# A retention layer in 64-token chunks with a carried state, interleaved with the two layers behind it

## The chip, the cores and the metric

The kernel runs on one core of a Trainium2 chip. The metric is the device time of one execution in microseconds (us), less is better. A core has TensorE (PE), VectorE (DVE), ScalarE (ACT), GpSimd (POOL) and SyncE (SP), each with its own instruction queue that is worked through in order; SP, ACT and POOL also issue DMAs. PEld in the profile is TensorE's loading of weights. SBUF is the on-chip memory, PSUM the memory that matmuls write.

## What is computed

A retention layer (attention without softmax, with a decay per head and a causal mask), then two linear layers with a leaky relu between them. 8 batches, 8 heads, 576 tokens, 64 elements per head, so 4608 tokens of width 512; the hidden width is 2048. Inputs and output are float32, and matmuls run in float16.

```python
scores = scale * np.matmul(q, k.transpose(0, 1, 3, 2))
gamma = 1.0 - 2.0 ** (-5.0 - np.arange(H, dtype=np.float32))
rel = pos[:, None] - pos[None, :]
Dmat = np.where(rel >= 0, gamma[:, None, None] ** rel[None, :, :], 0.0)
x = np.matmul(scores * Dmat[None], v)   # then heads side by side: (4608, 512)
h = x @ w_in                            # (4608, 2048)
g = np.maximum(0.01 * h, h)
out = g @ w_out                         # (4608, 512)
```

## The kernel before

It has two phases, one after the other, and a scheduler sets the order within each engine.

*Before the phases* it loads both weight matrices in float32 over SP's queue (lines 70 and 75) and casts them to float16 on DVE and ACT (71, 77, 79).

*Phase A* (lines 89 to 220) is the retention. It walks over 8 batches x 4 pairs of heads, 32 steps. Two heads share the 128 partitions: `kdiag` and `vdiag` hold the two heads' 64x64 blocks on the diagonal, so that one matmul serves both. A step loads q, k and v of a pair (SP and POOL), casts them (ACT line 130, POOL 131 and 135, ACT 136), transposes q and k on PE (141, 142), and copies the transposes out (145, 147, 151). Then it goes over nine blocks i of 64 keys. A matmul gives the scores of block i with all queries from block i on (185, 200), DVE multiplies them with a table of decays that is zero above the diagonal (192, 207), and two matmuls, which trail by two blocks, add the result times v into `oT0` and `oT1` (163, 170). ACT copies these into `xT` (218, 219), the transposed input of the first layer. So every query block meets every earlier key block.

*Phase B* (lines 222 to 280) goes over nine groups of 512 tokens. For each of 16 blocks `fc` of the hidden width four matmuls make `hps` (235). The leaky relu takes two operations: ACT makes 0.99 relu(h) (243), and DVE adds 0.01 h (247). The second layer's four matmuls of block fc - 1 follow (259), into four PSUM tiles; after the last block they are closed (268), ACT evicts them (277), and SP stores them.

Of the kernel before, what the change touches and what calls it, by code (L numbers as in the profile page):

```python
# [10 lines left out]
FP = mybir.dt.float32  # L11
F16 = mybir.dt.float16


@with_exitstack
def kernel(
# [8 lines left out]
):  # L25
    nc = tc.nc
# [4 lines left out]
    scale = 1.0 / np.sqrt(D)  # L31

    NPAIR = H // 2
    NW = (S + P - 1) // P
    NB = S // 64
    NC = DM // P
    NF = DFF // P
    TOK_G = 512
    NGRP = NT // TOK_G
    NTB = TOK_G // P  # L40

    gamma = 1.0 - 2.0 ** (-5.0 - np.arange(H, dtype=np.float64))
    r_idx = np.arange(P)[:, None]
    c_idx = np.arange(S)[None, :]
    ftab = np.zeros((NPAIR, P, S), dtype=np.float32)
    for p in range(NPAIR):
        gh = np.where(r_idx < 64, gamma[2 * p], gamma[2 * p + 1])
        rr = r_idx % 64
        expo = c_idx - rr
        ftab[p] = np.where(expo >= 0, gh ** np.maximum(expo, 0) * scale, 0.0)  # L50
    f_dram = nc.inline_tensor(ftab.astype(np.float16), name="f2_table")

    const_pool = ctx.enter_context(tc.tile_pool(name="const", bufs=1))
    xt_pool = ctx.enter_context(tc.tile_pool(name="xt", bufs=1))
    w_pool = ctx.enter_context(tc.tile_pool(name="w", bufs=1))
    stage_pool = ctx.enter_context(tc.tile_pool(name="stage", bufs=2))
    diag_pool = ctx.enter_context(tc.tile_pool(name="diag", bufs=1))

    ident16 = const_pool.tile([P, P], F16, name="ident16")
    make_identity(nc, ident16)  # L60

    f2_sb = const_pool.tile([P, NPAIR, S], F16, name="f2_sb")
    nc.sync.dma_start(out=f2_sb, in_=f_dram.ap().rearrange("h a t -> a h t"))

    xT = [xt_pool.tile([P, NT], F16, name=f"xT{r}") for r in range(DM // P)]

    w_in16 = [w_pool.tile([P, DFF], F16, name=f"w_in16_{c}") for c in range(NC)]
    for c in range(NC):
        st = stage_pool.tile([P, DFF], FP, name="w_in_stage")
        nc.sync.dma_start(out=st, in_=moe_w_in[c * P : (c + 1) * P, :])  # L70
        nc.vector.tensor_copy(out=w_in16[c], in_=st)
    w_out16 = [w_pool.tile([P, DM], F16, name=f"w_out16_{f}") for f in range(NF)]
    for f in range(NF):
        st = stage_pool.tile([P, DM], FP, name="w_out_stage")
        nc.sync.dma_start(out=st, in_=moe_w_out[f * P : (f + 1) * P, :])
        if f % 2 == 0:
            nc.scalar.copy(out=w_out16[f], in_=st)
        else:
            nc.vector.tensor_copy(out=w_out16[f], in_=st)

    qk16s = [diag_pool.tile([P, 2, NW, P], F16, name=f"qk16_{z}") for z in range(2)]
    kdiags = [diag_pool.tile([P, 2, NW, P], F16, name=f"kdiag{z}") for z in range(2)]
    vdiags = [diag_pool.tile([P, NB, P], F16, name=f"vdiag{z}") for z in range(2)]
    for z in range(2):
        nc.gpsimd.memset(qk16s[z][64:128, :, 4, :], 0.0)
        nc.gpsimd.memset(kdiags[z], 0.0)
        nc.gpsimd.memset(vdiags[z], 0.0)

    with ExitStack() as phA:
        in_pool = phA.enter_context(tc.tile_pool(name="inp", bufs=2))  # L90
        q2_pool = phA.enter_context(tc.tile_pool(name="q2", bufs=2))
        s2_pool = phA.enter_context(tc.tile_pool(name="s2", bufs=4))
        trq_pool = phA.enter_context(tc.tile_pool(name="trq", bufs=1, space=bass.MemoryType.PSUM))
        trk_pool = phA.enter_context(tc.tile_pool(name="trk", bufs=1, space=bass.MemoryType.PSUM))
        sc_pool = phA.enter_context(tc.tile_pool(name="sc", bufs=2, space=bass.MemoryType.PSUM))
        o0_pool = phA.enter_context(tc.tile_pool(name="o0", bufs=2, space=bass.MemoryType.PSUM))
        o1_pool = phA.enter_context(tc.tile_pool(name="o1", bufs=2, space=bass.MemoryType.PSUM))

        ipb = 0
        for b in range(B):  # L100
            for p in range(NPAIR):
                z = ipb % 2
                hA = 2 * p
                qk_sb = in_pool.tile([P, 2, NW, P], FP, name="qk_sb")
                vd32 = in_pool.tile([P, NB, D], FP, name="vd32")
                for ti, t_ap in enumerate((q, k)):
                    for hh in range(2):
                        nc.sync.dma_start(
                            out=qk_sb[:, ti, 0:4, 64 * hh : 64 * hh + 64],
                            in_=t_ap[b, hA + hh, 0:512, :].rearrange(  # L110
                                "(w t) d -> t w d", t=P
                            ),
                        )
                    nc.sync.dma_start(
                        out=qk_sb[0:64, ti, 4, :].rearrange("t (h d) -> t h d", h=2),
                        in_=t_ap[b, hA : hA + 2, 512:S, :].rearrange(
                            "h t d -> t h d"
                        ),
                    )
# [191 lines left out]
```

## Time and profile before

| | us |
|---|---|
| median of 3 runs (490.32 to 491.0) | 490.34 |
| span of the profiled execution | 488.2 |
| PE busy / DVE / ACT / POOL | 399.5 / 255.2 / 226.6 / 87.5 |
| phase A and loads, by the timeline | 0 to about 211 |
| phase B, by the timeline | about 211 to 484 |

The profile is one execution; a span counts from its first to its last instruction. Matmuls are pipelined and their ends modelled, so the distance between starts, not the busy time of one, says what a matmul costs in a row. In a group's row "xN | busy, mean | idle <-releaser", the idle time is what the engine waited just before these instructions, and the releaser is what ended most of it.

### The profile page before, as it was taken

The numbers are of one execution on the slowest core, as the hardware profiler recorded it, in microseconds if no ns is written. First come the engines' busy times: TensorE is split into PE (matmuls) and PEld (weight loads), VectorE is DVE, ScalarE is ACT, GpSimd is POOL, SyncE is SP. The second block draws the span as 40 slices with busy tenths as digits, with TensorE's granted clock in tenths as the row PEclk, the third lists the DMA queues.
The fourth block names the chain that finished last, engine by engine and source line by source line (L and its number), as shares of the span: only waits on it lengthen the run. The fifth ranks groups of instructions, "written<-read, shape, count | busy, mean of one in ns | idle before, by whom it ended". The sixth has DMA issues, their size and how long they took to land.

```text
span 488.2 us, 6567 instructions
## 1 busy us (share of the span) xinstructions
PE 399.5 (82%) x2336; PEld 203.8 (42%) x2336; DVE 255.2 (52%) x508; ACT 226.6 (46%) x381; POOL 87.5 (18%) x140
## 2 busy tenths in 40 slices
PE   0045788888888888889989899898999989899895
PEld 0023454545555555544434344343444434344341
DVE  2245688888887888883333333333333334334342
ACT  1145567666666666533343433434343343433433
POOL 8212344445444454200000000000000000000000
PEclk9998799999999999999999999999999999999999
DMA  8998798976767766100020200202001020200202
GB/s 305 263 241 215 167 190 190 192 162 149 161 165 165 155 160 160 37 0 1 0 86 2 86 1 1 86 1 86 1 23 64 0 87 1 85 2 0 86 1 86
DMA packets 89520, 47.16 MB, mean 97 GB/s; under 512 B 78736, under 2 KB 80272, under 8 KB 88976
## 3 DMA queue, kind: packets, MB, share of 16 engines
q1 hardware_dynamic: 85392, 37.31, 30.4%
q0 software_dynamic: 4096, 9.44, 7.1%
q8 instruction: 18, 0.29, 0.3%
q14 instruction: 14, 0.11, 0.1%
HBM read 37.29 MB, written 9.44 MB: 96 GB/s over the span
## 4 chain that ended last, share of the span: by engine, by line
PE 67%; DVE 13%; ACT 8%; DMA 5%; issue 3%; SPq 2%; ACTq 0%; DVEq 0%
PE opsum L259 24%; PE hps L235 23%; PE sc L200 10%; DVE s L207 6%; PE oT L163 4%; DVE s L192 4%; ACT qT L145 4%; DMA w_out_stage<-in_moe_w_out_dram 3%; ACT osb L277 2%; PE sc L185 2%; PE trQ L141 2%; DMA w_in_stage<-in_moe_w_in_dram 2%; DVE gt L247 1%; ACT rl L243 1%; PE oT L170 1%
## 5 line engine op out<-in xcount | busy, mean ns | idle before, releaser
L247 DVE SCALAR_TENSOR_TENSOR gt<-hps,rl 128x512 f16<-128x512 f32 x144 | 98.9, 691 | 164.5 <-ACT rl L243 164.2
L243 ACT ACTIVATE rl<-hps 128x512 f16<-128x512 f32 x144 | 85.5, 602 | 154.5 <-PE hps L235 154.5
L259 PE MATMUL opsum<-w_out,gt 128*128 128x512 f16 x540 | 138.5, 379 | 13.8 <-DVE gt L247 13.2
L235 PE MATMUL hps<-xT,w_in 128*128 128x512 f16 x576 | 148.6, 379 | 0.8 <-DVE gt L247 0.8
L207 DVE TENSOR_TENSOR s<-sc,f_sb 128x512 f16<-128x512 f32 (+7 forms) x256 | 106.3, 456 | 14.2 <-PE sc L200 13.7
L200 PE MATMUL sc<-qT,kdiag 128*128 128x512 f16 (+7 forms) x256 | 69.6, 292 | 21.9 <-DVE s L192 11.0
L259 PEld LDWEIGHTS <-gt 128*128 128x128 f16 x540 | 51.8, 97 | 79.8 <-DVE gt L247 38.0
L235 PEld LDWEIGHTS <-w_in 128*128 128x128 f16 x576 | 56.1, 98 | 67.8 <-issue 0.7
L163 PE MATMUL oT<-s,vdiag 128*128 128x512 f16 (+7 forms) x256 | 75.0, 294 | 0.1
L170 PE MATMUL oT<-s,vdiag 128*128 128x64 f16 x288 | 55.8, 195 | 0.4
L141 PE MATMUL trQ<-ident,qk 128*128 128x128 f16 x160 | 22.1, 226 | 34.8 <-ACT qk L130 27.6
L145 ACT COPY qT<-trQ 128x640 f16<-128x640 f16 x32 | 22.2, 692 | 49.5 <-PE oT L170 41.3
L163 PEld LDWEIGHTS <-vdiag 128*128 128x128 f16 x256 | 24.8, 98 | 29.5 <-issue 14.4
L130 ACT CAST qk<-qk_sb 128x1024 f16<-128x1024 f32 x32 | 33.5, 1046 | 6.7 <-DMA qk_sb<-in_k_dram 6.1
L200 PEld LDWEIGHTS <-kdiag 128*128 128x128 f16 x256 | 25.4, 99 | 26.1 <-issue 16.4
L192 DVE TENSOR_TENSOR s<-sc,f_sb 128x512 f16<-128x512 f32 x64 | 26.3, 453 | 17.6 <-PE sc L185 17.6
L135 POOL CAST vdiag<-vd 64x576 f16<-64x576 f32 x32 | 21.5, 673 | 71.9 <-PE oT L170 66.8
L170 PEld LDWEIGHTS <-vdiag 128*128 128x128 f16 x288 | 26.3, 98 | 10.8 <-issue 1.2
L141 PEld LDWEIGHTS <-qk 128*128 128x128 f16 x160 | 13.4, 101 | 40.7 <-ACT qk L130 28.4
L120 POOL DMA_DIRECT2D vd<-in_v_dram x32 | 23.8, 744 | 28.2 <-issue 11.1
L124 POOL DMA_DIRECT2D vd<-in_v_dram x32 | 24.3, 760 | 0.6 <-issue 0.5
L277 ACT COPY osb<-opsum 128x512 f32<-128x512 f32 x36 | 18.5, 599 | 10.9 <-PE opsum L268 10.9
(25 smaller groups left out, 177.6 us busy)
## 6 DMA issues: line engine op xcount, KB each, us to landing
vd<-in_v_dram POOLq DMA_DIRECT2D x64, 144.0 KB, 3.5
out_dram<-osb SPq DMA_DIRECT2D x36, 256.0 KB, 2.4
qk_sb<-in_q_dram SPq DMA_DIRECT2D x64, 128.0 KB, 3.5
qk_sb<-in_k_dram SPq DMA_DIRECT2D x64, 128.0 KB, 3.1
w_in_stage<-in_moe_w_in_dram SPq DMA_DIRECT2D x4, 1024.0 KB, 7.4
w_out_stage<-in_moe_w_out_dram SPq DMA_DIRECT2D x16, 256.0 KB, 3.0
qk_sb<-in_q_dram SPq DMA_DIRECT2D x32, 32.0 KB, 3.5
qk_sb<-in_k_dram SPq DMA_DIRECT2D x32, 32.0 KB, 2.7
```

Source lines behind the costliest of these rows:

```text
L130: nc.scalar.copy(out=qk16[:, :, 0:4, :], in_=qk_sb[:, :, 0:4, :])
L141: nc.tensor.transpose(trQ[:, w, :], qk16[:, 0, w, :], ident16)
L145: nc.scalar.copy(out=qT2, in_=trQ)
L163: nc.tensor.matmul(out=oT0[:, 64 * pi : 512], lhsT=vdiag[:, pi, :], rhs=s2_tiles[pi][:, 64 * pi : 512], start=(pi == 0), stop=(pi == 7),)
L170: nc.tensor.matmul(out=oT1[:, 0:64], lhsT=vdiag[:, pi, :], rhs=s2_tiles[pi][:, 512:S], start=(pi == 0), stop=(pi == NB - 1),)
L192: nc.vector.tensor_tensor(out=s2[:, a0:a1], in0=sc[:, 0 : a1 - a0], in1=f2_sb[:, p, a0:a1], op=mybir.AluOpType.mult,)
L200: nc.tensor.matmul(out=sc[:, 0 : S - n0], lhsT=kdiag[:, j, w, :], rhs=qTv[:, n0:S], start=True, stop=True,)
L207: nc.vector.tensor_tensor(out=s2[:, n0:S], in0=sc[:, 0 : S - n0], in1=f2_sb[:, p, 0 : S - n0], op=mybir.AluOpType.mult,)
L235: nc.tensor.matmul(out=hps, lhsT=w_in16[c][:, fc * P : (fc + 1) * P], rhs=xT[c][:, tok0 : tok0 + TOK_G], start=(c == 0), stop=(c == NC - 1),)
L243: nc.scalar.activation(out=rl, in_=hps, func=mybir.ActivationFunctionType.Relu, scale=0.99)
L247: nc.vector.scalar_tensor_tensor(out=gt, in0=hps, scalar=0.01, in1=rl, op0=mybir.AluOpType.mult, op1=mybir.AluOpType.add,)
L259: nc.tensor.matmul(out=opsum[tb], lhsT=g_tiles[pf][:, tb * P : (tb + 1) * P], rhs=w_out16[pf], start=(pf == 0), stop=False,)
```

## The change

Everything between the constants and the end of the kernel is new.

*Retention.* A head's 576 tokens are cut into nine chunks of 64. Within a chunk the scores are computed as before, with a 0/1 mask. All earlier chunks enter through a 64x64 state per head, the sum of k times v, which PSUM accumulates over three chunks (`ups`) and DVE then scales and carries on (`sinit`). The decay is no table on the scores: q and k are multiplied by powers of gamma when they are cast (`cast`), relative to the middle of a block of 192 tokens. The work is cut into 40 *units*, each 128 tokens of one batch over all eight heads (the last of a batch has 64).

*Loads.* Weights and v come by POOL's DMA queue, which casts them to float16 on the way. q and k come by SP's, four units ahead.

*Layers.* The leaky relu is one ACT operation. The second layer of a group runs during the first layer of the next; its output is evicted by DVE.

*Order.* The scheduler is off; each engine runs in program order. A unit is five slots (`slots`): s0 (loads, casts for later units, transposes), state of its first chunk, scores, state of its second, output. Units 0 to 3 run first, alone. Then round g = 0 to 9 has 16 blocks of layer 1 of group g and 16 of layer 2 of group g - 1, with the slots that group g + 1 needs spread between them.

Cut to its core:

```diff
-        for b in range(B):
-            for p in range(NPAIR):
...
-                nc.scalar.activation(
-                    out=rl, in_=hps, func=mybir.ActivationFunctionType.Relu, scale=0.99
-                )
...
+    ctx.enter_context(tc.manual_schedule())
...
+    def load_v(b):
+        t = v_pool.tile([P, NP, NI, D], F16, name="vst")
+        vst[b] = t
+        for p in range(NP):
+            for hh in range(2):
+                nc.gpsimd.dma_start(
+                    out=t[CH * hh : CH * hh + CH, p, :, :],
+                    in_=v[b, 2 * p + hh].rearrange("(i s) d -> s i d", s=CH),
+                )
...
+            eng = nc.vector if (u < 5 and x == 1) else nc.gpsimd
+            eng.tensor_tensor(
+                out=t[0:n],
+                in0=qk32[u, x][0:n],
+                in1=tab_sb[0:n, w % 3, x, :].unsqueeze(2).to_broadcast([n, H, D]),
+                op=MUL,
+            )
...
+    def st_transpose(u):
...
+        for hh in range(2):
+            nc.vector.tensor_copy(
+                out=vdiags[z][CH * hh : CH * hh + CH, :, 0:nb, CH * hh : CH * hh + CH],
...
+            for j in range(nb):
+                for hh in range(2):
+                    nc.vector.tensor_copy(
+                        out=kstks[z][CH * hh : CH * hh + CH, :, j, CH * hh : CH * hh + CH],
...
+        tr = tr_pool.tile([P, 2, NP, P], F16, name="tr")
+        for x in range(2):
+            for p in range(NP):
+                nc.tensor.transpose(
...
+        nc.scalar.copy(out=qT[:, :, 0:n], in_=tr[:, 0, :, 0:n])
+        for hh, eng in ((0, nc.scalar.copy), (1, nc.vector.tensor_copy)):
+            eng(
+                out=kdiags[z][CH * hh : CH * hh + CH, :, 0:nb, CH * hh : CH * hh + CH],
...
+    def st_state(u, j):
...
+        for p in range(NP):
+            nc.tensor.matmul(
+                out=ut[:, p, :],
+                lhsT=kstks[z][:, p, j, :],
+                rhs=vst[b][:, p, i, :],
...
+            if nxt % 3 == 0:
+                nc.vector.tensor_copy(out=dst, in_=sins[b][lo:hi])
+            elif nxt < 3:
+                nc.vector.tensor_copy(out=dst, in_=ut[lo:hi])
+            else:
+                nc.vector.tensor_tensor(out=dst, in0=ut[lo:hi], in1=sins[b][lo:hi], op=ADD)
+
+    def st_scores(u):
...
+        for p in range(NP):
+            for j in range(nb):
+                nc.tensor.matmul(
+                    out=sc[:, p, j, :],
+                    lhsT=kdiags[z][:, p, j, :],
+                    rhs=qTs[u][:, p, CH * j : CH * j + CH],
...
+            nc.vector.tensor_tensor(
+                out=s16.rearrange("s p j t -> s (p j) t"),
+                in0=sc.rearrange("s p j t -> s (p j) t"),
+                in1=mb.to_broadcast([P, NP * 2, CH]),
...
+    def st_out(u):
...
+                nc.tensor.matmul(
+                    out=o, lhsT=vdiags[z][:, p, j, :], rhs=s16s[u][:, p, j, :],
+                    start=True, stop=(i == 0),
+                )
+                if i > 0:
+                    nc.tensor.matmul(
+                        out=o, lhsT=sdiag_at[b, i][:, p, :],
...
+        nc.scalar.copy(out=xT[:, :, t0 : t0 + n], in_=ot[:, :, 0:n])
+
+    def slots(u):
...
+        def s0():
+            if u + 4 < NU:
+                load(u + 4)
+            if w == 1 and b + 1 < B:
+                load_v(b + 1)
+            if u + 2 < NU:
+                cast(u + 2)
+            st_transpose(u)
+
+        yield s0
+        yield lambda: st_state(u, 0)
+        yield lambda: st_scores(u)
+        if nrows[u] == P:
+            yield lambda: st_state(u, 1)
+        yield lambda: st_out(u)
...
+    load(0)
+    load_v(0)
+    for u in range(1, 4):
+        load(u)
+    cast(0)
+    cast(1)
+    FQ = DFF // 4
+    for c in range(4):
+        nc.gpsimd.dma_start(
+            out=w_in16[:, :, c * FQ : (c + 1) * FQ],
...
+    def g1(g, fc):
...
+        nc.scalar.activation(
+            out=g_tiles[g][:, fc, :], in_=hps,
+            func=mybir.ActivationFunctionType.Lrelu,
+        )
...
+    def g2(g, n):
+        tb, part = n // 4, n % 4
...
+        for f in range(4 * part, 4 * part + 4):
+            nc.tensor.matmul(
+                out=y_cur[g],
+                lhsT=g_tiles[g][:, f, tb * P : (tb + 1) * P],
...
+        if part == 3:
+            osb = o_pool.tile([P, DM], FP, name="osb")
+            nc.vector.tensor_copy(out=osb, in_=y_cur[g])
...
+    run_slots(ends[0])
+    for g in range(NG + 1):
...
+        for n in range(NF):
+            if g < NG:
+                g1(g, n)
+                m += 1
+                run_slots(a + (e - a) * m // nblk)
+            if g > 0:
+                g2(g - 1, n)
+                m += 1
+                run_slots(a + (e - a) * m // nblk)
```

*POOL, near the start of the program.* Before, POOL issued the v loads and cast parts of q, k and v; a name in brackets is a semaphore that is waited for (DMASW0 to 7 count POOL's own DMAs, DMAHW those of SP and ACT).

```order
L87 MEMSET vdiag_166 128x1152
L120 DMA vd_198<-in_v_dram 64x9x64
L124 DMA vd_198<-in_v_dram 64x9x64
L120 DMA vd_288<-in_v_dram 64x9x64
L135 CAST vdiag_165<-vd_198 64x9x64 [waits DMASW0_49]
L124 DMA vd_288<-in_v_dram 64x9x64
L135 CAST vdiag_166<-vd_288 64x9x64 [waits DMASW2_49,Pool_49]
```

In the changed kernel the same place reads as follows. `vst` is v of a batch, 170 is q of unit 2, 244 q of unit 3.

```order
L110 DMA vst<-in_v_dram 64x9x64 x8
L142 TENSOR_TENSOR qk_0_150<-qk_0_125,cs 128x512 [waits DMAHW1_49,DMAHW0_49]
L142 TENSOR_TENSOR qk_0_154<-qk_0_138,cs 128x512 [waits DMAHW3_49]
L325 DMA w_in_101<-in_moe_w_in_dram 128x4x512 [waits DMASW0_49]
L330 DMA w_out_102<-in_moe_w_out_dram 128x4x512 [waits DMASW7_49]
L142 TENSOR_TENSOR qk_0_170<-qk_0_142,cs 128x512 [waits DMAHW5_49]
L110 DMA vst<-in_v_dram 64x9x64 [waits DMASW0_49]
L110 DMA vst<-in_v_dram 64x9x64 [waits DMASW7_49]
L142 TENSOR_TENSOR qk_0_244<-qk_0_146,cs 128x512 [waits DMAHW7_49,PE_49,Pool_49]
```

The weight loads moved from SP to POOL, and stand between the v loads of batch 0 and those of batch 1 (first and last of each are shown). The eight semaphores are shared: each v load of batch 1 waits for the weight load that used its semaphore, and unit 3's q stands behind the last of them.

*ACT, in the middle of the program.* Before, in phase A, it ran one step's copies after another, and in phase B sixteen activations and four evictions, in turn.

```order
L145 COPY qT_1123<-trQ 128x640
L218 CAST xT_77<-oT_947 128x512
L219 CAST xT_77<-oT_948 128x64
L136 CAST vdiag_165<-vd_1098 64x9x64
L147 COPY kdiag_163<-trK 64x10x64
L130 CAST qk_0_161<-qk_sb 128x2x512
```

Now activations of layer 1 (`gt`) and the three copies of a unit alternate.

```order
L359 ACTIVATE gt<-hps 128x512
L184 COPY qT<-tr 128x512
L186 COPY kdiag_103<-tr 64x8x64
L359 ACTIVATE gt<-hps 128x512 x3
L286 CAST xT<-ot 128x4x128
```

The casts of q, k and v have left ACT; the copies of a unit stand among three to five activations.

*DVE, for one unit in the middle of the program.* Before, a step was a copy and ten masks of shrinking width.

```order
L151 COPY kdiag_164<-trK 64x10x64
L192 TENSOR_TENSOR s_1759<-sc,f_sb 128x512
L192 TENSOR_TENSOR s_1759<-sc,f_sb 128x64
L207 TENSOR_TENSOR s_1766<-sc,f_sb 128x512
L207 TENSOR_TENSOR s_1770<-sc,f_sb 128x448
```

Now a unit has these (`qk_1_2530` is its k in float16; `sdiag` the state in float16).

```order
L162 COPY vdiag_108<-vst 64x8x64 x2
L170 COPY kstk_106<-qk_1_2530 64x4x64 [waits Pool_49]
L170 COPY kstk_106<-qk_1_2530 64x4x64 x3
L186 COPY kdiag_104<-tr 64x8x64 [waits PE_49,Activation_49]
L233 TENSOR_TENSOR sdiag_111<-ups,sinit 64x4x64 [waits PE_49]
L233 TENSOR_TENSOR sdiag_111<-ups,sinit 64x4x64
L253 TENSOR_TENSOR s_2808<-sc,cs 128x512 [waits PE_49]
L222 TENSOR_TENSOR stmp<-ups,sinit 128x256 [waits PE_49]
L223 TENSOR_TENSOR sinit<-stmp,cs 128x256 [waits DVE_49]
L229 CAST sdiag_109<-sinit 64x4x64 [waits DVE_49]
L380 COPY osb<-yps 128x512 [waits DMAHW3_49,PE_49]
```

One mask of 128x512 per 128 tokens of all heads is left; eight to eleven small copies and sums for the block diagonals and the state, and the evictions of the output, have come.

More of the change, by code (lines that the diff above doesn't have):

```diff
@@ L62 @@
[L62 to L82, printed above, removed]
```

417 lines of the change are left out of this document (216 added, 201 removed).

## The prediction

> **What bounds the kernel now.** I read the page's head first, then the busy time in five stretches, then the chain that ended last, then the groups by shape.
>
> ```profile
> span 488.2 us, 6567 instructions
> PE 399.5 (82%) x2336; PEld 203.8 (42%) x2336; DVE 255.2 (52%) x508; ACT 226.6 (46%) x381; POOL 87.5 (18%) x140
> ```
>
> ```profile
> 0.00:30.00 30.00, 1.32 (x10) 0.91 (x10) 5.98 (x7) 5.79 (x8) 14.31 (x23) 1.00 0.93 280
> 30.00:60.00 30.00, 18.98 (x127) 11.60 (x128) 18.48 (x43) 16.44 (x28) 7.01 (x12) 0.83 0.81 198
> 60.00:211.00 151.00, 123.00 (x1004) 77.23 (x1004) 125.76 (x300) 100.21 (x163) 66.20 (x106) 1.00 0.71 154
> 211.00:484.00 273.00, 256.19 (x1196) 114.02 (x1194) 105.00 (x161) 104.06 (x184) 0.00 (x0) 1.00 0.09 32
> ```
>
> The columns are PE, PEld, DVE, ACT and POOL busy, granted clock, DMA share and GB/s. 82% of PE hides two kernels in a row. Up to 211 us the retention runs and TensorE waits for others; from 211 to 484 us the two layers run and TensorE is nearly full. The timeline in the first stretch and the chain in the second say how each is paced.
>
> ```profile
> 129.38 0.69 ACT L145 COPY qT<-trQ 128x640 f16<-128x640 f16 x1 [1.78 <-PE oT L170]
> 131.80 3.30 DVE L207 TENSOR_TENSOR s<-sc,f_sb 128x512 f16<-128x512 f32 x8 [0.34 <-PE sc L200]
> 134.93 0.69 ACT L145 COPY qT<-trQ 128x640 f16<-128x640 f16 x1 [1.79 <-PE oT L170]
> ```
>
> One head pair starts 5.55 us after the other, 3.30 us of it VectorE's masks, which no matmul of the layers covers: 32 pairs are 178 us.
>
> ```profile
> 275.01 0.31 PE opsum L268
> 277.26 0.65 ACT rl L243
> 277.93 0.70 DVE gt L247
> 278.68 1.04 PE opsum L259 x4
> 281.44 0.86 PE hps L235 x4
> ```
>
> In the layers four 128x512 matmuls take 0.86 us, **0.216 us each**, so a group of 128 is 27.6 us. Between groups the path leaves PE for evictions and the two-step leaky relu (275.3 to 278.7). The next such drain is at 304.5, so a group costs 29.5 us. So the layers lose little; what can be won is the first 211 us.
>
> **The change part by part.** The retention's arithmetic shrinks: 64-token chunks and a 64x64 state per head replace all pairs of chunks. Its PE work becomes 320 transposes and 1089 matmuls of 64 columns, placed in program order between the layers' 1152 matmuls. What do they cost?
>
> ```profile
> 130.47 0.44 PE L142 MATMUL trK<-ident,qk 128*128 128x128 f16 x5
> 134.65 0.19 PE L200 MATMUL sc<-qT,kdiag 128*128 128x64 f16 x1
> 134.68 0.22 PE L163 MATMUL oT<-s,vdiag 128*128 128x128 f16 x1
> 134.73 0.19 PE L170 MATMUL oT<-s,vdiag 128*128 128x64 f16 x1
> ```
>
> Five transposes take 0.44 us, one alone 0.22, so each further one adds **0.055 us**. After a 64-column matmul the next starts 0.03 us later, each with its own weight load. No row shows a long run of 64-column matmuls; bounds are 0.028 and the transposes' 0.056. I take 0.028, since its row has the shape.
>
> The Trainium skill, "TensorE: Matmul & The Clock Gate", section "Back-to-back issue gap", speaks against this: pairs of weight load and matmul sustain about 81 ns at 128 columns. The trace has 55 ns for just such pairs, so the measurement decides; by the page's figure the transposes of rounds 1 to 7 would add an estimated 6 us.
>
> *Head.* The program first runs units 0 to 3 (a unit is 128 tokens of all heads) without any layer work. POOL's order decides here: unit 3's q is scaled by a POOL instruction that stands behind the eight v loads of the next batch, and these wait for the semaphores of the eight weight loads. So **layer 1 cannot start before all 8.39 MB of weights have landed**. With them come q and k of units 0 to 3 (2.10 MB), v of batch 0 (1.18) and q, k of units 4 to 6 (1.31): 12.98 MB.
>
> ```profile
> q1 hardware_dynamic: 85392, 37.31, 30.4%
> q0 software_dynamic: 4096, 9.44, 7.1%
> ```
>
> At 280 GB/s, the first stretch's rate, that is 46 us; at 198, the second's, 66 us. The weights now come by POOL's queue with a cast in flight, which no row shows; q0, the same queue without a cast, moved 9.44 MB in 7.1% of 488.2 us, 272 GB/s. I take 50 us. Then follow one v issue, the scaling, and unit 3 in the open.
>
> ```profile
> L120 POOL DMA_DIRECT2D vd<-in_v_dram x32 | 23.8, 744 | 28.2 <-issue 11.1 <-POOL qk L131 10.6 <-ACT vdiag L136 5.0
> L135 POOL CAST vdiag<-vd 64x576 f16<-64x576 f32 x32 | 21.5, 673 | 71.9 <-PE oT L170 66.8 <-DMA vd<-in_v_dram 5.1
> L131 POOL CAST qk<-qk_sb 64x256 f16<-64x256 f32 x32 | 12.8, 401 | 19.2 <-PE trK L142 9.3 <-DMA qk_sb<-in_k_dram 9.3 <-PE sc L200 0.6
> ```
>
> ```profile
> 29.63 0.59 ACT qT L145
> 30.23 0.59 ACT kdiag L147
> 30.92 0.51 DVE kdiag L151
> 31.47 0.62 PE sc L185 x2
> 32.11 0.70 DVE s L192
> ```
>
> POOL's casts grow by 0.85 ns per element, so 512 take 0.62 us with one input; with two, between that and double, 1.24: I take 1.2, as the second input is read too. The old chain's first pair spent 3.2 us from qT to the mask (29.63 to 32.82); with transposes and 16 output matmuls at a clock not yet granted (0.9 each) and the copy to xT (0.6), and 0.4 of hand-overs, 6.0. Head: 50 + 0.7 + 1.2 + 6.0 = **58 us** (54 to 74).
>
> *Rounds 1 to 7* (a round is one pass over layer 1 of a group and layer 2 of the one before, with the next group's units between): 896 big matmuls x 0.216 = 193.5; their 31 units have 248 transposes x 0.056 = 13.9 and 828 small ones x 0.028 = 23.2. Sum 230.6, or 7.4 us per unit. Do the other engines keep up?
>
> ```profile
> L243 ACT ACTIVATE rl<-hps 128x512 f16<-128x512 f32 x144 | 85.5, 602 | 154.5 <-PE hps L235 154.5
> L247 DVE SCALAR_TENSOR_TENSOR gt<-hps,rl 128x512 f16<-128x512 f32 x144 | 98.9, 691 | 164.5 <-ACT rl L243 164.2 <-issue 0.3
> L218 ACT CAST xT<-oT 128x512 f16<-128x512 f32 x32 | 18.9, 590 | 7.2 <-PE oT L163 4.2 <-PE oT L170 3.0
> L192 DVE TENSOR_TENSOR s<-sc,f_sb 128x512 f16<-128x512 f32 x32 | 22.1, 692 | 17.6 <-PE sc L185 17.6
> L207 DVE TENSOR_TENSOR s<-sc,f_sb 128x256 f16<-128x256 f32 x32 | 13.6, 424 | 0.9 <-PE sc L200 0.8
> L79 DVE CAST w_out<-w_out_stage 128x512 f16<-128x512 f32 x8 | 3.8, 471 | 8.2 <-DMA w_out_stage<-in_moe_w_out_dram 8.1
> L151 DVE COPY kdiag<-trK 64x640 f16<-64x640 f16 x32 | 15.8, 495 | 5.9 <-ACT kdiag L147 5.0
> ```
>
> ACT per unit: 3.6 activations x 0.60 and three copies x 0.59: 4.0 us. The leaky relu loses its VectorE half, 144 x 0.691 = 98.9 us; I price the one-op form at L243's 602 ns. DVE per unit: two vdiag copies x 0.47, four kstk copies x 0.34 (between half of L79 and all of it), kdiag 0.43, four state halves x 0.42, the mask 0.69, a third of a carry 0.3, an output eviction 0.54: 6.1 us (5 to 7). POOL per unit: two scalings and 1.6 v issues, 3.7 us. All stay under 7.4, so **PE becomes the bound**, with small waits: from the transposes to the scores the path runs ACT, ACT, DVE, 0.8 + 0.59 + 0.5 + 0.5 = 2.4 us, where two layer blocks and the state matmuls cover 2.3. I charge 0.3 us per unit, 9 us. At each round's start layer 1 waits for the last unit's copy to xT: 0.2 + 0.59 + 0.1, eight times 0.95, 7.6 us. The second-layer matmuls now trail by a whole round, so L247's old drain is gone. Rounds 1 to 7: **247.5 us**.
>
> *Round 0* has only 64 layer matmuls (13.8 us) for units 4 to 8 (40 transposes, 136 small: 6.0), so its slots stand closer than the chain needs: about 1.2 us of wait per unit, 6 us, and 1.7 for the clock: 27.5. *Round 8* has no units, 27.6; *round 9* is 64 matmuls, 13.8.
>
> *Tail.*
>
> ```profile
> 481.59 1.04 PE L268 MATMUL opsum<-w_out,gt 128*128 128x512 f16 x4 [0.55 <-DVE gt L247]
> ```
>
> PE ended at 482.6 and the span at 488.2, 5.6 us later with four evictions, of which the first overlaps PE; I take 0.7 us off for three fewer, 4.9.
>
> **Sum:** 58 + 27.5 + 247.5 + 27.6 + 13.8 + 4.9 = 379.3 us of span against 488.2. The median of the runs shown, 490.34, is 2.1 above that span, so **381 us**.
>
> **The rivals.**
> *A: the casting weight loads are slow.* Nothing bounds them but q0. At half its rate, 136 GB/s, 8.39 MB take 31 us more: 412. For it: a cast is unseen; against: reads are in 2 KB rows, longer than q's 256 bytes.
> *B: small matmuls cost 0.056.* 964 of them outside the head add 27 us: 408. Against: the 0.03 us rows.
> *C: the cover fails, so the order does not do what it says.* If DVE or POOL trails, each unit shows 1 to 2 us more of its chain: 31 x 1.5 = 46, 427. POOL's scalings beside DVE's f16 copies could do it: were DVE held for both (2 x 1.2), it would need 8.5 us per unit against 7.4, and 31 x 1.1 + 12 in round 0 gives 427 as well. The trace has POOL and DVE busy together from 60 to 211 us (66 and 126 us) and cannot show this, as its POOL copies meet VectorE ops on PSUM. The Trainium skill, "SBUF — State Buffer", section "Who interferes with whom", states just this rule: VectorE copies in a two-port mode and GpSimd block each other wholly.
> *D, the other side: slower than before.* The head is paid in the open, since nothing of the layers stands before the last weight load. If they finish after 50 + 109 = 159 us, which is 12.98 MB at 82 GB/s, the gain is gone; at 70 GB/s they finish at 185 us and the time is 516. q0's 272 GB/s speaks against it.
>
> **How the numbers follow.** Forecast (366 to 398) 0.62; A 0.12; B 0.10; C 0.10; D 0.02; weights early and waits nil, under 366, 0.04. The range 362 to 414 takes in the forecast, A and B and the near part of C, about 0.85. Within 0.2% of before (what a measurement can tell from no change) only if C and A add up: 0.01; faster 0.96; slower 0.03.
>
> **What would show it.** The first layer-1 matmul near 58 us, released by an xT copy, with POOL's v issues of batch 1 held by weight landings before it; a clock of 1.00 after; rounds of 35 us; small matmuls 0.028 us apart in runs; PE idle mostly at round starts; DVE near 6 us per unit. Wrong would be a first layer matmul after 75 us, DVE over 85% busy in a round, or PE waiting on POOL.

## The result, and the profile after

The changed kernel takes **366.41 us** (median of 4, 365.23 to 366.62) against 490.67 for the kernel before on the same chip: a ratio of 0.746, 95% interval 0.744 to 0.748. The profiled execution has a span of 364.9 us. The page's head, and the busy time by round:

```profile
span 364.9 us, 6523 instructions
PE 311.6 (85%) x2560; PEld 168.9 (46%) x2560; DVE 198.1 (54%) x492; ACT 144.2 (40%) x266; POOL 131.4 (36%) x153
```

```profile
50.54:81.41 30.87, 24.60 (x241) 14.09 (x241) 23.32 (x55) 17.52 (x32) 18.27 (x20) 0.94 0.87 118
81.41:319.38 237.97, 232.67 (x1972) 125.79 (x1972) 142.44 (x360) 109.18 (x205) 85.10 (x94) 1.00 0.54 94
319.38:360.98 41.60, 41.60 (x192) 18.67 (x191) 4.88 (x8) 9.55 (x16) 0.00 (x0) 1.00 0.14 51
```

The rows of the second view are round 0, rounds 1 to 7 and rounds 8 and 9, with the columns of the table in the prediction. From 81 us on TensorE waits for next to nothing. What is left stands ahead of it, in the head and in round 0. The sum of the prediction against the trace:

| term | predicted | measured |
|---|---|---|
| head, to the first layer-1 matmul | 58 | 50.5 |
| round 0 | 27.5 | 30.9 |
| rounds 1 to 7 | 247.5 | 238.0 |
| rounds 8 and 9 | 41.4 | 41.4 by starts |
| tail | 4.9 | 4.0 |
| span | 379.3 | 364.9 |

*The head.* The timeline around its end:

```profile
42.72 0.73 POOL L110 DMA_DIRECT2D vst<-in_v_dram  x1 [2.84 <-DMA w_out<-in_moe_w_out_dram]
43.47 1.05 POOL L142 TENSOR_TENSOR qk<-qk,cs 128x512 f16<-128x512 f32 x1
...
44.58 1.03 PE L177 MATMUL tr<-ident,qk 128*128 128x128 f16 x8 [7.18 <-POOL qk L142]
...
50.54 1.01 PE L352 MATMUL hps<-xT,w_in 128*128 128x512 f16 x2 [0.67 <-ACT xT L286]
```

Read from top to bottom this is the predicted path: POOL's last v issue is released by the last landing of w_out, then comes unit 3's scaling, its transposes, and 6.0 us later layer 1.

*The rounds.* TensorE's waits (us in total, times, longest), over the whole span; two other large ones, 15.8 us for POOL's `qk` and 8.1 put down to w_in, are all in the head:

```profile
PE ups L203 <- DVE kstk L170: 11.7, 5, 5.3
...
PE hps L352 <- ACT xT L286: 5.9, 9, 0.7
```

The second row is the round starts, 0.67 us each time. The first row has two waits in the head (5.3 and 2.0 us), two in round 0 (2.4 and 1.1) and one later (0.8). The timeline shows what is behind the larger one of round 0:

```profile
60.00 2.12 POOL L142 TENSOR_TENSOR qk<-qk,cs 128x512 f16<-128x512 f32 x2
...
60.99 2.34 DVE L162 COPY vdiag<-vst 64x512 f16<-64x512 f16 x2
62.01 2.22 POOL L142 TENSOR_TENSOR half<-qk,cs 64x512 f16<-64x512 f32 x2
63.35 2.46 DVE L170 COPY kstk<-qk 64x256 f16<-64x256 f16 x4
64.20 1.03 POOL L142 TENSOR_TENSOR qk<-qk,cs 128x512 f16<-128x512 f32 x1
65.37 0.29 PE L203 MATMUL ups<-vst,kstk 128*128 128x64 f16 x4 [2.42 <-DVE kstk L170]
```

Two vdiag copies take 2.34 us and four kstk copies 2.46 while POOL scales five times in a row. The next unit's rows have 0.59 for two vdiag copies, so the copies were not slow, they stood still. The groups of the page that answer to prices of the prediction:

```profile
L359 ACT ACTIVATE gt<-hps 128x512 f16<-128x512 f32 x144 | 86.0, 597 | 133.0 <-PE hps L352 131.8
...
L170 DVE COPY kstk<-qk 64x256 f16<-64x256 f16 x128 | 34.2, 267 | 3.0
...
L162 DVE COPY vdiag<-vst 64x512 f16<-64x512 f16 (+1 forms) x80 | 27.0, 337 | 1.5
```

### The profile page after: what moved, and what is told of

Its sections match the earlier page's. It is cut to its first block, busy times and chain, and to the rows that moved or that the text cites. A ratio compares the mean times of both kernels' runs of the same rounds, so it can differ in the third digit from the quotient of the medians.

```text
span 364.9 us, 6523 instructions
## 1 busy us (share of the span) xinstructions
PE 311.6 (85%) x2560; PEld 168.9 (46%) x2560; DVE 198.1 (54%) x492; ACT 144.2 (40%) x266; POOL 131.4 (36%) x153
## 3 DMA queue, kind: packets, MB, share of 16 engines
q1 hardware_dynamic: 80192, 28.32, 35.2%
q0 software_dynamic: 42112, 8.92, 27.3%
HBM read 36.76 MB, written 9.44 MB: 127 GB/s over the span
## 4 chain that ended last, share of the span: by engine, by line
PE 78%; DMA 7%; DVE 6%; POOL 4%; ACT 2%; issue 2%; POOLq 0%; DVEq 0%
PE yps L371 34%; PE hps L352 32%; DMA w_out<-in_moe_w_out_dram 7%; PE tr L177 4%; PE ot L275 2%; PE sc L242 2%; PE ot L280 2%; POOL vst L110 2%; PE ups L203 2%; ACT xT L286 1%; DVE kstk L170 1%; POOL qk L142 1%; POOL w_in L325 1%; DVE s L253 1%; DVE sdiag L233 1%
## 5 line engine op out<-in xcount | busy, mean ns | idle before, releaser
L371 PE MATMUL yps<-w_out,gt 128*128 128x512 f16 x576 | 145.2, 379 | 0.0
L359 ACT ACTIVATE gt<-hps 128x512 f16<-128x512 f32 x144 | 86.0, 597 | 133.0 <-PE hps L352 131.8
L142 POOL TENSOR_TENSOR qk<-qk,cs 128x512 f16<-128x512 f32 x60 | 62.5, 1059 | 117.0 <-DMA qk<-in_q_dram 39.5
L110 POOL DMA_DIRECT2D vst<-in_v_dram x64 | 47.5, 775 | 32.8 <-DMA w_out<-in_moe_w_out_dram 11.4
L380 DVE COPY osb<-yps 128x512 f32<-128x512 f32 x36 | 24.9, 691 | 51.3 <-PE yps L371 51.0
L203 PE MATMUL ups<-vst,kstk 128*128 128x64 f16 x256 | 18.9, 199 | 21.1 <-DVE kstk L170 11.7
L170 DVE COPY kstk<-qk 64x256 f16<-64x256 f16 x128 | 34.2, 267 | 3.0
L177 PE MATMUL tr<-ident,qk 128*128 128x128 f16 x256 | 21.5, 232 | 15.8 <-POOL qk L142 15.8
L233 DVE TENSOR_TENSOR sdiag<-ups,sinit 64x256 f16<-64x256 f32 x64 | 26.9, 421 | 4.2 <-PE ups L203 3.3
L162 DVE COPY vdiag<-vst 64x512 f16<-64x512 f16 (+1 forms) x80 | 27.0, 337 | 1.5
L275 PE MATMUL ot<-s,vdiag 128*128 128x64 f16 x288 | 23.0, 199 | 2.6 <-DVE s L253 2.6
L275 PEld LDWEIGHTS <-vdiag 128*128 128x128 f16 x288 | 20.9, 102 | 5.6 <-issue 1.0
## 6 DMA issues: line engine op xcount, KB each, us to landing
w_in<-in_moe_w_in_dram POOLq DMA_DIRECT2D x4, 512.0 KB, 12.5
```

What stands on the lines that cost most here:

```text
L110: nc.gpsimd.dma_start(out=t[CH * hh : CH * hh + CH, p, :, :], in_=v[b, 2 * p + hh].rearrange("(i s) d -> s i d", s=CH),)
L142: eng.tensor_tensor(out=t[0:n], in0=qk32[u, x][0:n], in1=tab_sb[0:n, w % 3, x, :].unsqueeze(2).to_broadcast([n, H, D]), op=MUL,)
L162: nc.vector.tensor_copy(out=vdiags[z][CH * hh : CH * hh + CH, :, 0:nb, CH * hh : CH * hh + CH], in_=vst[b][CH * hh : CH * hh + CH, :, 2 * ...
L170: nc.vector.tensor_copy(out=kstks[z][CH * hh : CH * hh + CH, :, j, CH * hh : CH * hh + CH], in_=k16[CH * j : CH * j + CH, :, hh, :],)
L177: nc.tensor.transpose(tr[:, x, p, :], qk16[u, x][:, 2 * p : 2 * p + 2, :].rearrange("t h d -> t (h d)"), ident,)
L203: nc.tensor.matmul(out=ut[:, p, :], lhsT=kstks[z][:, p, j, :], rhs=vst[b][:, p, i, :], start=(i % 3 == 0 and p == 0), stop=(i % 3 == 2), s ...
```

## The experiments

Each was timed in three rounds beside the kernel before. Ratios are to that kernel.

| run | us | ratio (95%) |
|---|---|---|
| the change | 366.41 | 0.746 (0.744 to 0.748) |
| E1 v issued later | 364.20 | 0.741 (0.740 to 0.743) |
| E2 all units first | 500.67 | 1.019 (1.017 to 1.022) |
| E3 before, one-op leaky relu | 479.28 | 0.975 (0.972 to 0.977) |
| E4 the change, two-op leaky relu | 396.19 | 0.805 (0.803 to 0.807) |
| E5 slots two blocks earlier | 365.46 | 0.744 (0.742 to 0.745) |
| E6 E5, kstk copies on ACT | 377.16 | 0.767 (0.766 to 0.769) |
| E7 loads in order of need | 361.05 | 0.735 (0.734 to 0.736) |
| E9 E5 and E7 | 358.86 | 0.731 (0.728 to 0.733) |
| E11 E9, v behind the scaling | 358.05 | 0.730 (0.727 to 0.732) |
| E12 E11, scalings on DVE | 360.19 | 0.734 (0.732 to 0.735) |
| E13 E11, w_out and v moved again | 355.96 | 0.725 (0.723 to 0.726) |
| E14 the change, scalings twice | 388.16 | 0.789 (0.787 to 0.792) |

### What the gain is made of: E2, E3, E4

**E2** keeps every instruction and takes the interleaving away.

```diff
-    run_slots(ends[0])
+    run_slots(total)
```

> All 40 units run before the first layer-1 matmul; every instruction is kept, only the interleaving is gone. Theory (the gain is the hiding, not the smaller retention): in the open one unit follows the other by 6.35 us (units 1 and 2 in the head: 31.09 to 37.44), units of 64 tokens somewhat faster, so the layers start near 267 to 280 us, and 1152 matmuls of 0.216 us and a tail of 4 make 520 to 533 us: slower than the kernel before. Rival (the smaller retention carries most of the gain): below 430 us. Between them, 440 to 500, both would have a share.

Measured 500.67 us, 1.9% *slower* than the kernel before. The windows of E2: the units 4 to 39 (about), and the layers.

```profile
50.50:244.40 193.90, 100.53 (x1246) 81.95 (x1246) 169.23 (x387) 53.72 (x107) 104.02 (x114) 1.00 0.67 97
244.40:498.90 254.50, 250.58 (x1156) 112.80 (x1152) 24.91 (x36) 87.62 (x146) 0.00 (x0) 1.00 0.10 38
```

The theory holds, and the time is 19 us under its range: a unit in the open takes 193.9 / 36 = 5.4 us, not 6.35, with VectorE busy 87% of that stretch. So the smaller retention, by itself, is no gain here: at these rates 40 units are 215 us, where the old 32 pairs, 5.55 us each, were 178. It ends at 244.4 us, while the old one let the layers start at 213.5; one long chain per unit, of small steps on four engines, costs more in the open than fewer and larger steps did. The layers behind it take 254.5 us to the end of the span where the kernel before took 274.7 (213.5 to 488.2), which gives part of it back. All of the 124 us, and 10 more, come from hiding the units: 500.67 - 366.41 = 134 us. What hiding the old retention would have given, no run shows. It would need more of TensorE, which was busy with it for 123 of 151 us (60 to 211); the 31 units of rounds 1 to 7 take some 38 us (248 transposes 0.056 us apart, 828 small matmuls 0.029 apart).

**E3** and **E4** put the one-op leaky relu into the kernel before, and the two-op form into the change.

```diff
-                rl = g_pool.tile([P, TOK_G], F16, name="rl")
-                nc.scalar.activation(
-                    out=rl, in_=hps, func=mybir.ActivationFunctionType.Relu, scale=0.99
-                )
...
+                nc.scalar.activation(
+                    out=gt, in_=hps, func=mybir.ActivationFunctionType.Lrelu
+                )
```

> The kernel before with the one-op leaky relu alone. Theory (TensorE bounds the layers, and VectorE's half of the leaky relu stands on the path only at the nine group ends): 9 x 0.7 = 6 us less, 482 to 486. Rival (it counts for nothing, since the output evictions on ACT take the place of the drain): 489 to 491. Rival (the 98.9 us of VectorE were worth much more): below 475.

Measured 479.28, 12.5 us less, twice what was expected and under the theory's range. TensorE's waits in E3; the kernel before had 13.2 us, 8 times, longest 1.6, for VectorE's half (L247) at this place:

```profile
PE opsum L250 <- ACT gt L243: 2.2, 8, 0.3
```

So the wait at a group's start is the right place. A group became 1.39 us shorter (starts 29.52 us apart, then 28.13), not 0.70: VectorE's step is 0.69 of it, and in E3 the scheduler also leaves two blocks of layer 1 before the wait (eight matmuls in a row) where the kernel before had one. The runs don't take these two apart.

```diff
-        nc.scalar.activation(
-            out=g_tiles[g][:, fc, :], in_=hps,
-            func=mybir.ActivationFunctionType.Lrelu,
-        )
+        rl = o_pool.tile([P, TOK], F16, name="rl")
+        nc.scalar.activation(
+            out=rl, in_=hps, func=mybir.ActivationFunctionType.Relu, scale=0.99
+        )
+        nc.vector.scalar_tensor_tensor(
+            out=g_tiles[g][:, fc, :], in0=hps, scalar=0.01, in1=rl,
+            op0=MUL, op1=ADD,
+        )
```

> The changed kernel with the old two-op leaky relu: its VectorE half comes back, 144 x 0.691 = 99.5 us. Theory (the one-op form matters for the interleaving, because VectorE would otherwise be as full as TensorE): VectorE had 17 to 25 us of work in rounds 1 to 7 of 33.2 to 35.6 us; with 16 x 0.69 = 11.0 more it has 28 to 36, so rounds with five units are bound by it and the others wait now and then: 375 to 395 us. Rival (TensorE stays the bound, the second layer trails by a round and hides the longer path): 365 to 370. Rival (VectorE's 99 us come back whole): above 440.

Measured 396.19, 30 us more than the change and 1 us above the range. Round 0 and rounds 1 to 7 of E4, and TensorE's largest wait in these rounds:

```profile
52.35:90.74 38.39, 27.76 (x240) 14.66 (x240) 29.87 (x70) 16.43 (x31) 18.30 (x20) 0.87 0.63 86
90.74:349.66 258.92, 237.60 (x1972) 123.75 (x1972) 212.11 (x476) 109.30 (x205) 85.26 (x94) 1.00 0.50 87
```

```profile
PE ups L203 <- DVE kstk L170: 13.8, 18, 1.9
```

Rounds 1 to 7 take 21 us more, round 0 takes 7.5 more. VectorE is at 212 of 259 us in rounds 1 to 7, and the state matmuls wait there for `kstk` 18 times, where the change has one such wait of 0.8 us. The one-op form is worth 12.5 us in the old order and 30 in the new one: it makes the room in which the units are hidden.

### The head: E1, E7

**E1** issues v of a batch with unit 3 of the batch before, not unit 1.

```diff
-            if w == 1 and b + 1 < B:
+            if w == 3 and b + 1 < B:
```

> The v loads of batch 1 are issued two units later (with unit 3 instead of unit 1), so the scaling of unit 3's q on POOL no longer stands behind eight v issues that wait for the weights to land. Theory (POOL's order set the head): TensorE is free for unit 3 at 37.4 us, its chain takes the same 6.0, so the first layer-1 matmul comes at 43 to 44 us instead of 50.5 and the time falls by 5 to 7 us, to 359 to 361; the last 1 to 2 us may go to unit 5, whose v now lands near 48 us. Rival (the wait is only moved: unit 5 needs that v and its own scaling in round 0, and both stand behind the same landings): first layer-1 matmul early, but round 0 grows by the same, 364 to 367. Rival (the weights themselves are late): first layer-1 matmul stays near 50 us.

Measured 364.20, only 2.2 us less. Unit 3 is free and layer 1 starts at 41.7 us, 8.8 earlier, but round 0 takes 37.3 us, 6.4 more. The timeline of E1 in round 0:

```profile
51.28 0.88 DVE L162 COPY vdiag<-vst 64x512 f16<-64x512 f16 x1 [4.46 <-DMA vst<-in_v_dram]
...
54.38 0.40 PE L203 MATMUL ups<-vst,kstk 128*128 128x64 f16 x4 [5.37 <-DVE kstk L170]
```

VectorE stands 4.46 us for v of batch 1. The first rival is right: the wait behind the weights was real, but with it gone the next thing that stands behind the same 8.4 MB is late. What must change is the order of the bytes.

**E7** does that.

```diff
             if u + 2 < NU:
                 cast(u + 2)
+            if u == 0:
+                load_w_in()
+            if u == 3:
+                load_v(1)
+                load_w_out()
```

> The changed kernel with another order of loads: w_in is issued after the scaling of unit 2, and v of batch 1 and then w_out only with unit 3, so that what the head and round 0 need is read first. Theory (up to some 53 us the chip reads at its full rate of 300 GB/s, and only the order decides what is late): q, k of units 0 to 3 and v of batch 0 (3.3 MB) are there after 11 us, the four units run one after the other by 6.3 us, the first layer-1 matmul comes at 34 to 38 us, round 0 takes 27 to 31, and the time is 350 to 356 us. Rival (the bytes are all needed by the end of round 0 and are only late elsewhere: 17.6 MB by the start of round 1 take 59 us): round 1 waits for w_out, 358 to 364.

Measured 361.05 us. The head shrinks to 39.4 us, 11.1 less, and half of that is lost again: round 0 takes 36.3. But not as the rival has it, with round 1 waiting for w_out: rounds 1 to 7 take 237.8 us, as in the change. The timeline of E7 in round 0:

```profile
58.00 0.73 POOL L110 DMA_DIRECT2D vst<-in_v_dram  x1 [2.62 <-PE ups L203]
...
58.74 2.05 POOL L142 TENSOR_TENSOR qk<-qk,cs 128x512 f16<-128x512 f32 x2
...
60.35 6.71 DVE L223 TENSOR_TENSOR sinit<-stmp,cs 128x256 f32<-128x256 f32 x1
60.75 2.03 POOL L142 TENSOR_TENSOR half<-qk,cs 64x512 f16<-64x512 f32 x2
...
62.75 4.03 POOL L142 TENSOR_TENSOR qk<-qk,cs 128x512 f16<-128x512 f32 x4
...
69.76 0.40 PE L203 MATMUL ups<-vst,kstk 128*128 128x64 f16 x4 [7.52 <-DVE kstk L170]
```

One multiply of 128x256, which takes 0.42 us elsewhere in this trace, takes **6.71**. It stands through seven scalings and ends 0.3 us after the last of eight that POOL does without a pause. They had piled up behind v issues: two of these wait 1.1 and 2.6 us for w_out to land, and the last, 3.35 us after the one before it, is put down to a state matmul. TensorE waits 7.5 us for what VectorE does next, and its clock falls with it (0.86 over round 0).

### VectorE beside POOL: E14, E5, E6, E12

**E14** doubles the suspected cost in the change: every POOL scaling from unit 9 on is done twice.

```diff
+            if u >= 9:
+                nc.gpsimd.tensor_tensor(
+                    out=scr[0:n],
+                    in0=qk32[u, x][0:n],
...
+                )
```

> The changed kernel, with every POOL scaling from unit 9 on done a second time into a scratch tile that nothing reads: 62 more scalings of 1.04 us, so POOL has some 150 of the 238 us of rounds 1 to 7 instead of 85 and is still far from full. Theory (VectorE's copies and its operations with two operands in SBUF stand still while POOL scales): scalings stand in rows of four, one VectorE operation after another is stretched by 1 to 4 us, the state matmuls wait, and rounds 1 to 7 take 10 to 30 us longer: 376 to 396 us. Rival (what was stretched in round 0 was stretched by the loads, and POOL's work beside VectorE costs nothing): 365 to 369 us.

Measured 388.16 us, 21.8 more. Rounds 1 to 7, and one place in them:

```profile
86.47:340.36 253.89, 236.78 (x1972) 126.46 (x1972) 166.63 (x360) 109.23 (x205) 139.80 (x148) 0.99 0.50 88
```

```profile
221.74 6.97 DVE L170 COPY vdiag<-vst 64x512 f16<-64x512 f16 x2
...
227.20 1.05 POOL L150 TENSOR_TENSOR scr<-qk,cs 128x512 f16<-128x512 f32 x1
...
229.23 0.17 PEld L211 LDWEIGHTS <-kstk 128*128 128x128 f16 x4 [5.12 <-DVE kstk L178]
```

POOL is at 55% (139.8 of 253.9) and VectorE does the same 360 instructions, yet VectorE's busy time grows by 24 us and the rounds by 16. TensorE's largest wait in these rounds:

```profile
PE ups L211 <- DVE kstk L178: 12.6, 5, 4.6
```

It waits for none of POOL's own results there, so that the scalings come later is not what costs the time. From all records of a trace, the duration of VectorE's operations (mean, longest, ns) with no POOL scaling beside them and with one or more:

```
operation, operands                  the change                    E14
                                     without       with            without       with
vdiag copy, SBUF to SBUF             286,  610     697, 1287       276,  429    1465, 6711
kstk copy, SBUF to SBUF              229,  465     783, 1091       231,  480     946, 2025
multiply of sinit, two from SBUF     424,  425     744, 1299       424,  424     702, 1236
multiply of ups, one from PSUM       425,  425     425,  426       425,  425     425,  425
mask, one from PSUM                  691,  693     691,  693       691,  693     691,  693
sum for sdiag, one from PSUM         420,  428     421,  428       421,  429     421,  428
```

Operations that read PSUM never stretch; copies within SBUF and the multiply with both operands in SBUF do. The longest copies of the change in the column "without", 610 and 465 ns, stand beside v issues of POOL, so its DMA issues stretch them too; E13 has a larger case. With nothing of POOL's beside them no kstk copy of the change takes over 226 ns and no vdiag copy over 292. What the scalings do is what the Trainium skill says in "SBUF — State Buffer", section "Who interferes with whom": the two engines share one pair of SBUF ports, which copies in a two-port mode and operations with two SBUF inputs need, and one blocks the other wholly. The traces agree, down to which operations are hit. The page speaks of a wait for one instruction; here VectorE stood through seven of POOL's in a row (twice in E14, once in E7), in other places it got its turn after one.

**E5** ends each round's slots two blocks earlier.

```diff
+        nsl = max(nblk - 2, 1)
...
-                run_slots(a + (e - a) * m // nblk)
+                run_slots(a + (e - a) * min(m, nsl) // nsl)
```

> The slots of each round are spread over two blocks fewer, so that the last unit of a round has its copy to xT two blocks (1.7 us) before layer 1 of the next round begins. Theory (the round start waits for that copy alone, 0.67 us each): 8 x 0.67 = 5.4 us less, 360 to 361.5. Rival (the slots now stand closer than a unit's chain, and the waits come back inside the rounds): 365 to 368.

Measured 365.46, 0.95 less, with intervals that just overlap: in the rival's range. TensorE's waits in E5 over the whole span, and behind them the one from 83 to 325 us:

```profile
PE ups L203 <- DVE kstk L170: 27.4, 12, 8.7
...
PE hps L352 <- ACT xT L286: 0.7, 1, 0.7
```

```profile
PE ups L203 <- DVE kstk L170: 2.8, 6, 0.8
```

Eight of the nine waits at round starts are gone, as the theory says, and in rounds 1 to 7 the state matmuls wait for kstk six times, 2.8 us, where the change has 0.8 us once. These rounds fall by 2.7 us (238.0 to 235.3), half of what was expected. The head, where nothing was edited, grows by 1.8 us (50.5 to 52.3) and takes most of it back. (Of the 27.4 us, 8.6 are the head's first wait, which the change has too, with 8.1, put down to w_in.) In the head the copies of unit 3 and POOL's scalings come close together, and in this execution POOL came first:

```profile
41.56 5.11 DVE L162 COPY vdiag<-vst 64x512 f16<-64x512 f16 x2
...
42.47 1.05 POOL L142 TENSOR_TENSOR qk<-qk,cs 128x512 f16<-128x512 f32 x1
43.48 1.04 POOL L142 TENSOR_TENSOR half<-qk,cs 64x512 f16<-64x512 f32 x1
44.48 2.03 POOL L142 TENSOR_TENSOR qk<-qk,cs 128x512 f16<-128x512 f32 x2
```

**E6** takes the kstk copies from VectorE to ACT, on top of E5.

```diff
-                    nc.vector.tensor_copy(
+                    nc.scalar.copy(
                         out=kstks[z][CH * hh : CH * hh + CH, :, j, CH * hh : CH * hh + CH],
```

> As the run with the slots two blocks earlier (365.46 us), but the kstk copies run on ACT instead of VectorE; nothing else differs. Theory (VectorE's f16 copies wait while POOL scales, and that is what came back inside the rounds): the waits of the state matmuls for kstk go, 3.8 us in rounds 1 to 7 and 2 to 4 in round 0, so 357 to 361 us; the vdiag copies are still caught. Rival (ACT, with 128 x 0.37 = 47 us more, becomes late with the leaky relu and the xT copies): 366 or more. Rival (the waits have another cause, such as the distance of the slots): 364 to 366.

Measured 377.16, 11.7 more than E5: the first rival. TensorE's waits in E6:

```profile
PE sc L242 <- DVE kdiag L186: 31.6, 19, 8.8
...
PE ups L203 <- ACT kstk L170: 2.9, 8, 0.7
```

The wait for kstk went (27.4 to 2.9), but the copies now stand ahead of qT and kdiag in ACT's queue, and the scores wait for those (4.7 before). ACT is only 52% busy; its order, not its load, costs the time.

**E9** has both edits, E5's slots and E7's loads.

> Both edits: the loads in the order of need and the slots two blocks earlier. If they are independent, this is about 1 us under the run with the order of loads alone, as the slots alone gave (366.4 to 365.5): 349 to 355 us. If the waits that came back with the earlier slots hang on POOL scalings that stood piled up behind the weights, more of the 5.7 us of the round starts is kept: 345 to 350 us.

Measured 358.86, 2.2 under E7: more than the 1 us of independent edits, from a base that was 361 and not 350 to 356. Rounds 1 to 7 fall by 2.6 us (237.8 to 235.2), as they fall by 2.7 in E5; here the head stays as it was.

**E11** issues v behind the scaling, on top of E9.

```diff
-            if w == 1 and 0 < b and b + 1 < B:
-                load_v(b + 1)
             if u + 2 < NU:
                 cast(u + 2)
...
+            if w == 3 and b + 1 < B:
+                load_v(b + 1)
```

> As the run with loads in the order of need and early slots (358.86 us), but each batch's v loads are issued two units later and behind the scaling of that unit, so that no POOL scaling stands behind an issue that waits for w_out. Theory (the 7.7 us of wait near 62 to 69 us is VectorE kept from SBUF by eight POOL scalings in a row, which were piled up behind that issue): they no longer pile up, VectorE's sinit multiply, which took 6.7 us there, takes 0.42, and with the half clock that followed 8 to 9 us go: 349 to 352 us. Rival (VectorE or TensorE waited for the landing itself, of w_out or of v of batch 2): round 0 stays at 36 us, 357 to 360.

Measured 358.05: nothing beyond the measurement's width. The multiply, 6.71 us in E7 and 7.18 in E9, takes 0.87, so that pile is gone, but others stand elsewhere. The timeline of E11:

```profile
42.05 5.04 POOL L142 TENSOR_TENSOR qk<-qk,cs 128x512 f16<-128x512 f32 x5
...
43.85 3.72 DVE L162 COPY vdiag<-vst 64x512 f16<-64x512 f16 x2
...
48.13 0.29 PE L203 MATMUL ups<-vst,kstk 128*128 128x64 f16 x4 [2.25 <-DVE kstk L170]
```

Behind any long stretch on POOL, here the twelve issues of v and w_out from 32.3 to 42.0 us, scalings pile up. Round 0 is still 35.2 us.

**E12**, beside E11, gives the scalings from unit 9 on to VectorE.

```diff
-            eng = nc.vector if (u < 5 and x == 1) else nc.gpsimd
+            eng = nc.vector if ((u < 5 and x == 1) or u >= 9) else nc.gpsimd
```

> As the run before it in this list, but from unit 9 on the scalings of q and k run on VectorE, so that POOL computes nothing any more in rounds 1 to 7 and only issues loads. Theory (VectorE's copies wait for POOL's scalings, 3.4 us in rounds 1 to 7): these waits go, and VectorE, with 1.38 us more per unit, is at 6.4 of 7.4: 3 us less than the run before it. Rival (VectorE is now too full, its masks and sums come late): 2 to 10 us more.

Measured 360.19, 2.1 more than E11: the rival. Round 0 and rounds 1 to 7 of E12:

```profile
39.97:71.50 31.53, 23.82 (x240) 13.21 (x240) 24.73 (x61) 16.48 (x31) 14.20 (x17) 0.95 1.33 170
71.50:314.50 243.00, 233.57 (x1974) 123.86 (x1973) 167.00 (x416) 110.20 (x206) 29.29 (x40) 1.00 0.53 92
```

Round 0 fell by 3.7 us, where POOL's pile was; rounds 1 to 7 grew from 235.9 to 243.0, since two scalings of VectorE (1.28 us) now stand ahead of the vdiag and kstk copies for which TensorE waits. VectorE is at 69%: again the place in a queue, not the load.

### A version that beats both: E13

w_out is issued with unit 5, behind its scaling, and v two loads per slot.

```diff
-            if w == 3 and b + 1 < B:
-                load_v(b + 1)
-            if u == 3:
+            if u == 5:
                 load_w_out()
...
+        def with_v(p, f):
+            if w == 3 and b + 1 < B:
+                load_v(b + 1, [p])
+            f()
```

> As the run with v issued behind the scaling (358.05 us), with the v loads two per slot instead of eight in a row (6 us of POOL at once) and w_out issued with unit 5, behind its scaling. Theory (POOL's scalings keep VectorE out only when several stand in a row, and they pile up behind any long stretch of issues or of waiting on POOL): rows of four and five scalings in round 0 become rows of two, VectorE's 3.7 and 4.7 us copies shrink to 2 or less, round 0 falls from 35.2 to 30 to 32 us: 353 to 355 us. Rival (round 0 waits for its data, and the blocked copies only fill that time): round 0 stays at 34 to 35, 357 to 359; or w_out, issued later, holds up round 1.

Measured **355.96 us**, a ratio of 0.725 (0.723 to 0.726), 10 us under the change and just above the range. Its head, round 0, and rounds 1 to 7:

```profile
0.00:42.78 42.78, 12.78 (x156) 10.22 (x157) 32.24 (x68) 7.90 (x14) 26.15 (x37) 1.00 1.35 185
42.78:73.77 30.99, 25.10 (x241) 13.97 (x241) 24.66 (x57) 16.64 (x31) 20.29 (x23) 0.94 1.24 161
73.77:310.04 236.27, 232.94 (x1973) 124.49 (x1972) 142.52 (x359) 110.18 (x206) 85.17 (x94) 1.00 0.55 95
```

Round 0 fell by 4.2 us, to where the theory put it, but the head grew by 3.3, and the row of v issues was not broken up. POOL runs ahead of the slots, so the eight v issues still stood in a row, and they and the four scalings behind them now fall on unit 3:

```profile
33.69 5.95 POOL L111 DMA_DIRECT2D vst<-in_v_dram  x8
...
36.79 2.16 DVE L171 COPY kstk<-qk 64x256 f16<-64x256 f16 x1
```

That copy takes 0.23 us undisturbed, and only issues stand beside it. The rival's late w_out doesn't show. Round 0 still takes 11 us more than its matmuls (13.8 + 6.0 in the prediction); what a version without POOL's long stretches would take was not tried.

## Why the prediction was right, and where it was off

The forecast was 381 us in a range of 362 to 414; it took 366.4, near the lower end. The mechanism was right: TensorE became the bound from round 1 on. Four terms were mis-sized.

- **Head, 58 for 50.5.** Path and order were right, each step of it (1.05 for the scaling where 1.2 was taken, 6.0 for unit 3 in the open). The landing of the weights was the mis-sized term: "I take 50 us" was 12.98 MB at 260 GB/s, and they landed at 42.7, so at about 300 for the same bytes. Rival A falls: POOL's casting loads kept up. That the weights' landing holds unit 3 was right but no lever by itself (E1), because round 0 needs bytes that stand behind them.
- **Rounds 1 to 7, 247.5 for 238.0.** The pure matmul time of 230.6 was right: 238.0 less seven round starts (six at 0.84, the last at 0.63) and one wait of 0.96 leaves 231.3. So the small matmuls cost 0.029 us and rival B falls; there are 1088 of them in all, not 1089. "I charge 0.3 us per unit, 9 us" was the mis-sized step: the waits inside the rounds came to 1 us. VectorE had 142.4 / 31 = 4.6 us per unit, not 6.1 (the terms of that sum add to 5.9); undisturbed, its kstk and vdiag copies take 0.23 and 0.29 us, where 0.34 and 0.47 were taken from L79, a row that reads float32. The round starts were 0.84, not 0.95.
- **Round 0, 27.5 for 30.9.** Here rival C's mechanism acted, and the forecast had no term for it: the two waits for kstk, behind stretched copies, are 3.5 us, about what is missing. Rival C charged it to every unit, 427 us. In rounds 1 to 7 VectorE's operations were stretched too, to 1.3 us at most, but TensorE waited behind them once, 0.8 us; what cost time were scalings that stand in a row. E14, which makes such rows everywhere, costs 22 us.
- **Tail, 4.9 for 4.0**, and rounds 8 and 9 as predicted. The one-op leaky relu was priced at 602 ns and takes 597.
- **"What can be won is the first 211 us"** was right only through the hiding: E2 has the first phase 31 us longer than before. And the leaky relu is more than the group drains: E3 gives 12.5 us, E4 30 in the new order.

## What to carry to other kernels

Measure a rewritten phase once with the overlap taken away: here the new kernel is 10 us slower than the old one without the overlap and 124 faster with it, and that tells what must be kept when the order is edited. Before an instruction is moved to an engine with time to spare, look at what would stand behind it in that engine's queue: ACT at 40% and VectorE at 60% both lost time by it. Where POOL computes beside VectorE, keep its work from piling up behind waits and long rows of DMA issues.

## What the runs showed of the hardware that was not expected

A VectorE operation can stand through a row of seven of POOL's, 6.71 us for one of 0.29 or 0.42 (E14, E7); when it gets a turn in between differed from place to place. POOL's DMA issues keep it out as well, 2.16 us for a copy of 0.23 (E13). And v, cast in flight, goes in packets of 128 bytes, one for each of its 36864 rows; POOL's queue in the change:

```profile
q0 software_dynamic: 42112, 8.92, 27.3%
```

Before, it moved 9.44 MB, v in float32, in 4096 packets and 7.1% of the time of 16 engines. Now the 8.92 MB written, v and both weights in float16, take 42112 packets and 27.3% of a shorter span.
